# Moving the Q projection of eight token tiles from a fused attention/FFN kernel's K stage to the start of their FFN chunk

## The chip, the cores and the metric

The kernel runs on one core of a Trainium2 chip. The metric is the device time of one execution in microseconds. The core has TensorE for matmuls (PE in the profile, with PEld for its weight loads), VectorE (DVE) and ScalarE (ACT) for elementwise work, GpSimd (POOL), and SyncE (SP), whose queue issues the data transfers here. Matmul results go to PSUM, eight banks of 2 KB in each of 128 partitions; everything else lives in SBUF.

## The reference

One transformer block computes linear attention and a GeGLU feed-forward in parallel on the same normalized input; S = 2048 tokens, D = 576, 32 heads of 18, F = 4608, all in bf16:

```python
xn = layernorm(x)                       # over D, eps 1e-5
q, k, v = heads(xn @ wqkv)              # 32 heads of 18
phi = lambda t: where(t > 0, t + 1, exp(t)) + 1e-6
kv  = einsum("bhsd,bhse->bhde", phi(k), v)
z   = einsum("bhsd->bhd", phi(k))
num = einsum("bhqd,bhde->bhqe", phi(q), kv)
den = einsum("bhqd,bhd->bhq", phi(q), z)[..., None] + 1e-6
attn = merge_heads(num / den) @ wo
ffn  = (gelu(xn @ w_gate) * (xn @ w_up)) @ w_down
return x + attn + ffn
```

## The kernel before

The kernel works in two parts. In the **K stage** it goes over 16 tiles of 128 tokens. Each is normalized (statistics on VectorE, `rstd` on ScalarE, the scaling on either), transposed by a DMA (the first two by TensorE), projected to K and Q, and put through phi. From phi(K) it accumulates G = xn^T phi(K) in PSUM; a few steps after the last tile turn G and the V weights into the heads' kv products. Then come four **chunks** of 512 tokens. Each has 36 gate/up units (two outputs of 512 columns, gelu, product), and then the down projection of its four token tiles, into which the attention output is added.

The K and Q matmuls of a tile are ten each, of 288 columns: two halves of the 576 outputs, five blocks of the contraction. D = 576 is four blocks of 128 and a rest of 64, so the fifth block is half empty. Its row 64 (`HP`) holds ones on both sides, which adds 1 to the projection; phi is then max(t+1, min(exp(t), 1)), with the exponential's bias of -1:

```python
def kq_mm(n, which, hf):                        # which: 1 = K, 0 = Q
    c = which * D + hf * HALF
    for kt in range(KT):                        # KT = 5
        nc.tensor.matmul(                       # line 281
            ps_all[:, KQ_BANK[which] + hf, :HALF], lhsT=xnT[:, kt, n * P:(n + 1) * P],
            rhs=wqkv_sb[:, kt, c:c + HALF], start=(kt == 0), stop=(kt == KT - 1),
        )

def kq_exp(n, which, hf):                       # ScalarE, line 296
    ...activation(out=e, in_=ps_all[...], func=ACT.Exp, bias=neg1[:], scale=1.0)

def kq_phi(n, which, hf):                       # VectorE, line 301
    ...scalar_tensor_tensor(out=(pq, pk)[which][...], in0=e, scalar=1.0,
                            in1=ps_all[...], op0=ALU.min, op1=ALU.max)

def g_accumulate(n, pieces):                    # line 320; seven matmuls a tile in the K stage
    ...matmul(ps_all[:, b, col:col + w], lhsT=xn[:, n, kt * P:(kt + 1) * P],
              rhs=pk[:, n, 1 + d0:1 + d0 + w], ...)

def z_add(n):                                   # GpSimd, line 210: running sum of phi(K)
    ...tensor_tensor(out=z_sum, in0=z_sum, in1=pk[:, n, 1:D + 1], op=ALU.add)
```

`pk` has one column of ones on each side of a tile's phi(K), from which G also gets its column sums. Two matmuls of 289 columns a tile (`g_strip`, line 327) do G's 64-row rest.

The order in which the K stage's steps are given to the engines comes from a greedy model (`in_order`) with a duration for each step; a list `HEAD` fixes the first part of the order, up to about tile 5. Each engine runs its own steps in that order. Names in the list: `s` statistics, `a` aggregate, `r` rstd, `n` norm, `b` its bias, `t` a TensorE transpose, `c` the transposed tile, `m n.w.h` the matmuls of tile n, K (w = 1) or Q (w = 0), half h; `e` exponential, `p` phi, `z` the sum, `G`, `x` a load of two tiles, `w` warm-up matmuls.

The gate/up units run on two row tiles of TensorE: the upper and lower 64 rows of the array each hold their own weights, and two matmuls run side by side into two banks. For the rest of 64 rows, the lower half of the fifth block is a copy of the upper one:

```python
class _Unit:
    def p1(self):                               # first = (4, 0, 1, 2, 3): five pairs
        for kt in self.first:
            self.mm(0, LO, kt, ...)             # line 351
            last = self.mm(1, HI, kt, ...)
        self.turn = self.relay.nop()            # waits for `last`
    def p2(self):                               # then = (0, 1, 2, 3): four pairs, banks swapped
        for kt in self.then:
            m = self.mm(1, LO, kt, ...)         # the first waits for self.turn
            self.mm(0, HI, kt, ...)

def gu_pair(sc, k):                             # cut
    for i in range(GUB):                        # GUB = 2 units
        u = _Unit([bank a, bank b], lhs, rhs, nc.sync if blk == 0 else nc.gpsimd)
        u.p1()
    for each unit:
        u.p2()
        gelu on ScalarE (679), product to hT on VectorE (680)
    one job of den_jobs                         # phi(Q) -> normalized, transposed pqT
```

`den_jobs` uses phi(Q) of four tiles in each chunk, those of the chunk itself. After the K stage the transfers are issued in this order on one queue:

```python
load_w(2)                                       # V weights
nc.sync.dma_start(wqkv_sb[HP:P, 4, 2 * D:], A_wqkv[512:576, 2 * D:])
for i in range(NWBUF):                          # four blocks of gate/up weights
    load_gu(i, 0)
    load_gu(i, 1)
for c0, c1 in ((0, SC), (SC, S)):               # line 600
    nc.sync.dma_start(xnT[HP:P, 4, c0:c1], xnT[0:HP, 4, c0:c1])
for n in range(NS - 2):
    g_accumulate(n, G_B)                        # the fourth block's G
g_accumulate(NS - 1, G_A)
...                                             # copies of G, strips, kv products
```

At the end of each chunk but the last the tiles 2 and 3 of the down projection get one pair of matmuls (line 738) and then their adds on VectorE (764).

Of the kernel before, what the change touches and what calls it, by code (L numbers as in the profile page):

```python
# [15 lines left out]
P = 128  # L16
# [24 lines left out]
XW = 640  # L41
KLO = HP + 1
Q_CUT = 3
PKW = 578


class _Ring:
# [11 lines left out]
def kernel(  # L59
# [119 lines left out]
    nc.gpsimd.memset(xn[:, :, D:XW], 0.0)  # L179
    nc.gpsimd.memset(xn[:, :, D:D + 1], 1.0)  # L180
    nc.gpsimd.memset(wqkv_sb[HP:HP + 1, 4, 0:2 * D], 1.0)
    nc.gpsimd.memset(pk[:, :, 0:1], 1.0)
    nc.gpsimd.memset(pk[:, :, D + 1:D + 2], 1.0)

    bmask = const.tile([P, CR], F32, name="bmask")
    g_sb = apool.tile([P, KT, D], BF16, name="g_sb")
# [21 lines left out]

    def z_add(n):
        nc.gpsimd.tensor_tensor(  # L210
            out=z_bf[:] if n == NS - 1 else z_sum[:], in0=pk[:, 0, 1:D + 1] if n == 1 else z_sum[:], in1=pk[:, n, 1:D + 1],
            op=ALU.add,
        )

# [84 lines left out]

    def kq_phi(n, which, hf):  # L300
        nc.vector.scalar_tensor_tensor(  # L301
            out=(pq, pk)[which][:, n, which + hf * HALF:which + (hf + 1) * HALF], in0=e_tiles[n, which, hf][:], scalar=1.0,
            in1=ps_all[:, KQ_BANK[which] + hf, :HALF], op0=ALU.min, op1=ALU.max,
        )

    G_A = {
# [3 lines left out]
    }  # L312
    G_B = {3: [(4, 0, 0, 288), (5, 0, 288, 289)]}
    STRIP = ((6, 0, 1, 0), (7, HALF + 1, 0, HALF))
    eps_sum = const.tile([P, KT], F32, name="eps_sum")

    def g_accumulate(n, pieces):
        for kt, ps_ in pieces.items():
            for b, col, d0, w in ps_:
                nc.tensor.matmul(  # L320
                    ps_all[:, b, col:col + w], lhsT=xn[:, n, kt * P:(kt + 1) * P], rhs=pk[:, n, 1 + d0:1 + d0 + w],
                    start=(n == 0 and col == 0), stop=(n == NS - 1), skip_group_check=True,
                )

    def g_strip(n):
        for rows, (b, c0, _, _) in zip((LO, HI), STRIP):
            nc.tensor.matmul(  # L327
                ps_all[rows, b, 0:HALF + 1], lhsT=xn[:, n, 4 * P:D], rhs=pk[:, n, c0:c0 + HALF + 1],
                start=(n == 0), stop=(n == NS - 1), skip_group_check=True,
            )  # L330

# [126 lines left out]
    def step(name, *args, **kw):  # L458
        steps[name] = _Step(*args, **kw)

    GL = 0.0
    NORM = "DDDAADADADADADAD"
    COPY = ("DVE", "ACT")
    LEAD = (-9.0, 0.5, -0.5, -0.5)
    X_AT = [3.35, 4.40, 6.30, 8.80] + [10.40] * 4
# [4 lines left out]
    for n in range(NS):  # L470
        lead = LEAD[n] if n < 4 else 0.0
        after_x = [("x", n // 2 * 2)] if n >= 8 else []
        x_at = X_AT[n] if n < 8 else 0.0
        for h in range(2):
            step(("stats", n, h), "DVE", 0.40, n - 2.2 + lead, after_x, lambda n=n, h=h: ln_half(n, h), ready=x_at, tail=0.02)
        step(("aggr", n), "DVE", 0.14, n - 2.1 + lead, [("stats", n, 0), ("stats", n, 1)], lambda n=n: ln_aggr(n), tail=0.07)
        step(("rstd", n), "ACT", 0.43, n - 2.1 + lead, [("aggr", n)], lambda n=n: ln_rstd(n), tail=0.07)
        if n < TD:
            for i, (k0, k1, eng) in enumerate([(0, 3, "ACT"), (3, KT, COPY[n])]):
                b = TP_BANK[n] - i  # L480
                if NORM[n] == "A":
                    if not i:
                        step(("bias", n), "POOL", 0.20, n - 2.1 + lead, [("rstd", n)], lambda n=n: ln_bias(n))
                    step(("norm", n, i), "ACT", (0.49, 0.36)[i], n - 2.1 + lead, [("bias", n)],
                         lambda n=n, k0=k0, k1=k1: ln_norm_act(n, k0 * P, min(k1 * P, D)))
                else:
                    step(("norm", n, i), "DVE", (0.26, 0.19)[i], n - 2.1 + lead, [("rstd", n)],
                         lambda n=n, k0=k0, k1=k1: ln_norm(n, k0 * P, min(k1 * P, D)), tail=0.05)
                step(("tp", n, i), "PE", (0.32, 0.21)[i] if n == 0 else (0.18, 0.12)[i], n - 1.5 + lead, [("norm", n, i)],
                     lambda n=n, k0=k0, k1=k1, b=b: transposes(n, k0, k1, b), tail=0.08)  # L490
                step(("xnT", n, i), eng, 0.27 if i else 0.44, n - 0.88 + lead, [("tp", n, i)],
                     lambda n=n, k0=k0, k1=k1, b=b, eng=eng: tp_copy(n, k0, k1, b, acopy if eng == "ACT" else vcopy), tail=0.04)
            ready = [("xnT", n, 0), ("xnT", n, 1)]
        else:
            if NORM[n] == "P":
                step(("norm", n), "POOL", 2.35, n - 2.1 - GL, [("rstd", n)], lambda n=n: ln_norm_pool(n))
            elif NORM[n] == "A":
                step(("bias", n), "POOL", 0.15, n - 2.1, [("rstd", n)], lambda n=n: ln_bias(n))
                step(("norm", n), "ACT", 0.77, n - 2.1, [("bias", n)], lambda n=n: ln_norm_act(n), tail=0.09)
            else:  # L500
                step(("norm", n), "DVE", 0.36, n - 2.1, [("rstd", n)], lambda n=n: ln_norm(n), tail=0.07)
            step(("xnT", n), "SP", 2.10, n - 1.9, [("norm", n)], lambda n=n: dma_transposes(n), tail=2.05)
            ready = [("xnT", n)]
        for which, rank in ((1, n), (0, n + 0.6)):
            for h in range(2):
                r = rank + h / 100
                free = [("phi", n - 1, which, h)] if n else []
                if n == which == 0:
                    k0, k1 = ((0, Q_CUT), (Q_CUT, KT))[h]
                    step(("mm", 0, 0, h), "PE", 0.246 * (k1 - k0), r, ready + [("mm", 0, 0, 0)][:h],  # L510
                         lambda k0=k0, k1=k1: q_first(k0, k1), ready=W_AT[0][h], tail=0.15)
                else:
                    step(("mm", n, which, h), "PE", 0.615, r, ready + free, lambda n=n, w=which, h=h: kq_mm(n, w, h),
                         ready=W_AT[which] if which else W_AT[0][1], tail=0.15)
                step(("exp", n, which, h), "ACT", 0.46, r + 0.10, [("mm", n, which, 1 if n == which == 0 else h)],
                     lambda n=n, w=which, h=h: kq_exp(n, w, h), tail=0.03)
                step(("phi", n, which, h), "DVE", 0.37, r + 0.15, [("exp", n, which, h)],
                     lambda n=n, w=which, h=h: kq_phi(n, w, h), tail=0.08)
        if n > 0:
            idle = [("bias" if NORM[n + 4] == "A" else "norm", n + 4)] if n + 4 < NS else []  # L520
            step(("z", n), "POOL", 1.40, n + 2.0, [("phi", m, 1, h) for m in (0, n) for h in range(2)] + idle + ([("z", n - 1)] if n > 1 else []),
                 lambda n=n: z_add(n))
        step(("G", n), "PE", 0.75, n + 1.15, [("phi", n, 1, 0), ("phi", n, 1, 1)], lambda n=n: g_accumulate(n, G_A))
# [5 lines left out]
    def in_order(steps):  # L529
# [15 lines left out]
        return [name for _, _, name in sorted(begun)]  # L545

    HEAD = """
        s0.1 s0.0 a0 r0 s1.1 n0.0 t0.0 n0.1 t0.1 s1.0 a1 w c0.1 s2.0 c0.0 s2.1 m0.1.1 a2 r1 r2 m0.1.0 n1.1 e0.1.1
        t1.1 n1.0 n2 p0.1.1 m0.0.0 t1.0 B s3.0 e0.1.0 s3.1 a3 m0.0.1 c1.1 c1.0 e0.0.0 r3 m1.1.1 p0.1.0 p0.0.0 s4.1
        G0 m1.1.0 e0.0.1 s4.0 b3 c2 g n3 c3 e1.1.1 s5.0 p0.0.1 m1.0.0 e1.1.0 a4 p1.1.1 m1.0.1 s5.1 r4 p1.1.0 e1.0.0  # L550
        a5 m2.1.1 b4 e1.0.1 s6.0 m2.1.0 x8 s6.1 G1 n4 p1.0.0 e2.1.0 p1.0.1 m2.0.0 a6 e2.1.1 s7.0 p2.1.0 r5 m2.0.1
        p2.1.1 n5 z1 m3.1.0 c4 r6 s7.1 e2.0.1 e2.0.0 m3.1.1 G2 c5 p2.0.1 e3.1.0 a7 p2.0.0 p3.1.0 s8.0 b6 e3.1.1
        p3.1.1 z2 m3.0.1 s8.1 n6 a8 e3.0.1 s9.0 m3.0.0 c6 e3.0.0 G3 p3.0.1 s9.1 r7 a9 x10 n7 r8 m4.1.0 e4.1.0 x12
        m4.1.1 e4.1.1 m4.0.1 z3 r9 p3.0.0 m4.0.0 c7 p4.1.0 e4.0.1 p4.1.1 e4.0.0 n9 m5.1.0 p4.0.1 G4 b8 z4 m5.1.1 n8
        e5.1.0 c9
    """
    KIND = {
        "x": "x", "s": "stats", "a": "aggr", "r": "rstd", "b": "bias", "n": "norm", "t": "tp", "c": "xnT", "m": "mm",
# [87 lines left out]
    def gu_pair(sc, k):  # L646
# [29 lines left out]
        for i, (b, u) in enumerate(units):  # L676
# [4 lines left out]
            if den_jobs and i == 1 and 0 < k < NF // GUB - 1:  # L681
                job, n = den_jobs.pop(0)
                job(n)

    def m_product(c, bank):
        rows = DH * HCH[c]
        for hf in range(2):
# [80 lines left out]
                nc.sync.dma_start(out_view[:, self.n, :], self.res[:])  # L768

    for sc in range(NSC):  # L770
        for k in range(NF // GUB):
            gu_pair(sc, k)
            if sc == 0 and k in m_last_steps:
                m_last_steps[k]()
        while wd_loaded[0] < NF:
            load_wd_slice()

        tiles = [_DownTile(sc * TPC + j) for j in range(TPC)]
        tiles[0].pair()
        tiles[1].pair()  # L780
# [2 lines left out]
        for j, t in enumerate(tiles):  # L783
# [44 lines left out]
```

## Time and profile before

The time is 512.04 us (three executions, 512.02 to 512.2); the profiled execution spans 510.4 us.

| engine | busy us | share | what it mostly does |
|---|---|---|---|
| PE (TensorE) | 505.7 | 99% | pairs of gate/up, down projection, K and Q |
| PEld (weight loads) | 304.6 | 60% | runs beside PE |
| DVE (VectorE) | 212.7 | 42% | product of gate/up; statistics and phi in the K stage |
| ACT (ScalarE) | 137.0 | 27% | gelu; exponentials in the K stage |
| POOL (GpSimd) | 25.9 | 5% | sum of phi(K) |

A few groups of instructions matter for what follows (duration of one, from the page and the groups of the first 66 us): K/Q matmul 286 ns, 310 of them on line 281 and 10 on line 289 (the first tile's Q); exponential of 128x288 497 ns; phi 448 ns; statistics 444 ns; norm of 576 columns 860 ns on ScalarE and 696 ns on VectorE; sum of phi(K) on GpSimd 1249 ns; transposing DMA 1.2 us of issue and 2.6 us to landing.

A busy time is the sum of the recorded durations, with overlaps counted once. Instructions on one engine are pipelined: the next one starts before the record of the one before has ended, so the distance from start to start is what an instruction costs in a row. The chain of waits is followed back from the last instruction, at each step to what released it; a piece of it is the time by which the end would move if that piece alone went away and nothing else came in its place. A line such as 351 is that of a helper: gate/up and other units share it and are told apart by the tiles they read.

### The profile page before, as it was taken

How to read it: one execution, taken by the hardware profiler on the slowest of the kernel's cores; microseconds unless marked ns; L12 is line 12 of the kernel's file. 1: busy time of each engine (PE TensorE's matmuls, PEld its weight loads, DVE VectorE, ACT ScalarE, POOL GpSimd, SP SyncE). 2: the span in 40 equal slices, each digit the busy share in tenths (PEclk: the TensorE clock that was granted, in tenths of full speed). 3: DMA queues.
4: the chain of work that ended last, by engine and by line, in shares of the span. 5: the costliest groups of instructions: out<-in, count | busy, mean ns of one | idle time of the engine just before them, and what ended most of it. 6: DMA issues, size and time to landing. Idle time of an engine off the chain costs nothing.

```text
span 510.4 us, 10676 instructions
## 1 busy us (share of the span) xinstructions
PE 505.7 (99%) x4489; PEld 304.6 (60%) x4489; DVE 212.7 (42%) x449; ACT 137.0 (27%) x267; POOL 25.9 (5%) x40
## 2 busy tenths in 40 slices
PE   8999999999999999999999999999999999999997
PEld 7888854444587744444677644444777444445774
DVE  7996455555400045565210255555100356544101
ACT  6996523332400022322100023223000232232000
POOL 3444200000000000000000000000000000000000
PEclk9999999999999999999999999999999999999999
DMA  6747329999400067665300256567000556550000
GB/s 211 149 88 199 93 86 269 286 275 280 132 13 12 1 182 164 151 170 164 84 12 13 72 166 173 156 175 160 27 12 1 146 159 168 162 128 14 13 12 24
DMA packets 119162, 61.26 MB, mean 120 GB/s; under 512 B 25730, under 2 KB 118410, under 8 KB 119114
## 3 DMA queue, kind: packets, MB, share of 16 engines
q1 hardware_dynamic: 118970, 60.43, 45.4%
q8 instruction: 35, 0.57, 0.5%
q10 hardware_dynamic: 144, 0.15, 0.1%
q14 instruction: 13, 0.11, 0.1%
HBM read 52.86 MB, written 2.36 MB: 108 GB/s over the span
## 4 chain that ended last, share of the span: by engine, by line
PE 98%; DVE 1%; ACT 0%; DMA 0%; issue 0%
PE ps_all L351 55%; PE ps_all L750 28%; PE ps_all L281 7%; PE ps_all L320 3%; PE ps_all L755 3%; DMA x_sb<-in_A_x_dram 0%; PE ps_all L738 0%; PE ps_all L327 0%; DVE stats L224 0%; PE ps_all L400 0%; PE ps_all L690 0%; ACT phi_e L296 0%; ACT xnT L270 0%; DVE mv L227 0%; DVE xn L245 0%; ACT rstd L231 0%
## 5 line engine op out<-in xcount | busy, mean ns | idle before, releaser
L351 PE MATMUL ps_all<-xnT,wg 64*128 64x512 bf16 x1152 | 272.1, 376 | 0.0
L351 PE MATMUL ps_all<-xnT,wu 64*128 64x512 bf16 x1152 | 271.6, 376 | 0.0
L679 ACT ACTIVATE gl<-ps_all 128x512 f32<-128x512 f32 x144 | 86.0, 597 | 308.9 <-PE ps_all L351 308.8
L680 DVE TENSOR_TENSOR hT<-ps_all,gl 128x512 bf16<-128x512 f32 x144 | 99.6, 692 | 130.8 <-ACT gl L679 130.4
L351 PEld LDWEIGHTS <-wu 64*128 64x128 bf16 x1152 | 108.3, 94 | 68.1
L351 PEld LDWEIGHTS <-wg 64*128 64x128 bf16 x1152 | 108.3, 94 | 67.8
L750 PE MATMUL ps_all<-wd_sb,hT 128*128 128x288 bf16 (+2 forms) x1152 | 147.1, 286 | 0.0
L750 PEld LDWEIGHTS <-hT 128*128 128x128 bf16 x1152 | 110.9, 98 | 30.9 <-issue 1.3
L764 DVE TENSOR_TENSOR res<-ps_all,x_sb 128x288 bf16<-128x288 f32 (+2 forms) x32 | 13.8, 455 | 146.3 <-PE ps_all L755 88.1
L351 PE MATMUL ps_all<-xnT,wr 64*128 64x512 bf16 x288 | 54.6, 376 | 0.0
L281 PE MATMUL ps_all<-wqkv_sb,xnT 128*128 128x288 bf16 x310 | 40.7, 286 | 0.1
L281 PEld LDWEIGHTS <-xnT 128*128 128x128 bf16 x310 | 29.5, 98 | 7.3 <-ACT xnT L270 0.4
L296 ACT ACTIVATE phi_e<-ps_all,neg 128x288 f32<-128x288 f32 x64 | 30.7, 497 | 9.2 <-PE ps_all L281 6.2
L351 PEld LDWEIGHTS <-wr 64*128 64x128 bf16 x288 | 14.0, 94 | 16.7
L755 PE MATMUL ps_all<-m_sb,pqT 128*128 128x288 bf16 (+2 forms) x128 | 20.9, 286 | 0.0
L320 PE MATMUL ps_all<-hT,xn 128*128 128x288 bf16 (+4 forms) x144 | 18.8, 274 | 0.0
L210 POOL TENSOR_TENSOR z_sum<-z_sum,hT 128x576 f32<-128x576 f32 x13 | 16.2, 1249 | 18.5 <-DVE hT L301 17.8
L301 DVE SCALAR_TENSOR_TENSOR pq<-phi_e,ps_all 128x288 bf16<-128x288 f32 x32 | 14.1, 448 | 6.1 <-ACT phi_e L296 6.0
L320 PEld LDWEIGHTS <-xn 128*128 128x128 bf16 x144 | 13.9, 98 | 3.9 <-DVE hT L301 0.3
L301 DVE SCALAR_TENSOR_TENSOR hT<-phi_e,ps_all 128x288 bf16<-128x288 f32 x32 | 14.0, 448 | 2.6 <-ACT phi_e L296 2.4
L755 PEld LDWEIGHTS <-pqT 128*128 128x128 bf16 x128 | 12.4, 98 | 3.3
L224 DVE BATCH_NORM_STATS2 stats<-x_sb 128x6 f32<-128x288 bf16 x32 | 13.4, 444 | 1.1 <-DMA x_sb<-in_A_x_dram 1.1
(70 smaller groups left out, 130.7 us busy)
## 6 DMA issues: line engine op xcount, KB each, us to landing
wg<-in_B_w_gate_dram SPq DMA_DIRECT2D x72, 256.0 KB, 2.9
wu<-in_B_w_up_dram SPq DMA_DIRECT2D x72, 256.0 KB, 3.6
wd_sb<-in_B_w_down_dram SPq DMA_DIRECT2D x12, 432.0 KB, 4.8
wr<-in_B_w_gate_dram SPq DMA_DIRECT2D x72, 32.0 KB, 2.9
wr<-in_B_w_up_dram SPq DMA_DIRECT2D x72, 32.0 KB, 3.1
out_dram<-res SPq DMA_DIRECT2D x15, 144.0 KB, 1.8
wqkv_sb<-in_A_wqkv_dram SPq DMA_DIRECT2D x2, 576.0 KB, 4.5
x_sb<-in_A_x_dram SPq DMA_DIRECT2D x4, 288.0 KB, 3.6
```

The source lines that it names most:

```text
L210: nc.gpsimd.tensor_tensor(out=z_bf[:] if n == NS - 1 else z_sum[:], in0=pk[:, 0, 1:D + 1] if n == 1 else z_sum[:], in1=pk[:, n, 1:D + 1], ...
L224: nc.vector.bn_stats(out=ln_raw[n][:, h, :], in_=x_sb[:, n, h * HALF:(h + 1) * HALF])
L281: nc.tensor.matmul(ps_all[:, KQ_BANK[which] + hf, :HALF], lhsT=xnT[:, kt, n * P:(n + 1) * P], rhs=wqkv_sb[:, kt, c:c + HALF], start=(kt == ...
L296: nc.scalar.activation(out=e[:], in_=ps_all[:, KQ_BANK[which] + hf, :HALF], func=ACT.Exp, bias=neg1[:], scale=1.0,)
L301: nc.vector.scalar_tensor_tensor(out=(pq, pk)[which][:, n, which + hf * HALF:which + (hf + 1) * HALF], in0=e_tiles[n, which, hf][:], scala ...
L320: nc.tensor.matmul(ps_all[:, b, col:col + w], lhsT=xn[:, n, kt * P:(kt + 1) * P], rhs=pk[:, n, 1 + d0:1 + d0 + w], start=(n == 0 and col = ...
L351: return nc.tensor.matmul(self.outs[i], lhsT=self.lhs(i, rows, kt), rhs=self.rhs(i, rows, kt), start=start, stop=stop, skip_group_check=True,)
L679: nc.scalar.activation(out=gl[:], in_=ps_all[:, b[0], :], func=ACT.Gelu_apprx_tanh)
L680: nc.vector.tensor_tensor(out=hT[:, GUB * k + i, :], in0=ps_all[:, b[1], :], in1=gl[:], op=ALU.mult)
L750: nc.tensor.matmul(self.acc(hf), lhsT=hT[:, f, j * P:(j + 1) * P], rhs=wd_sb[:, f, self.parts[hf]], start=(f == 0 and not paired), stop=Fa ...
L755: nc.tensor.matmul(self.acc(hf), lhsT=pqT[:, c, self.ts], rhs=m_sb[:, c, self.parts[hf]], start=False, stop=(paired and c == 3), skip_grou ...
L764: nc.vector.tensor_tensor(out=self.res[:, hs], in0=self.acc(hf), in1=x_sb[:, self.n, hs], op=ALU.add)
```

## The change

Q of the tiles 6, 7, 9, 10, 11, 13, 14 and 15 is no longer computed in the K stage. It is computed at the start of the chunk to which the tile belongs (two tiles in chunk one, three each in chunks two and three), as units on two row tiles, like gate/up. The 64-row rest then is one pair. It uses no row of ones: phi is formed as max(t, 0) + min(exp(t), 1), with one more VectorE operation for each half. The Q weights are loaded a second time, into the buffer that held `wo`, after the first down tile of chunk zero. ScalarE loads its exponential table before the down projections of chunks zero to two, and that of gelu again after the late Q.

The whole K stage is now a fixed list of steps, with its Q halves of tiles 4, 5, 8 and 12 set behind later tiles' K. The model's number for the transposing DMA changes from 2.10 us to 1.25 (with a tail of 2.9 or 2.0 us), and the assignment of norms to engines becomes strictly alternating from tile 3. The store of phi(K) gets four columns of ones on each side instead of one, so that a tile begins on a multiple of four elements; G's last pieces and its strips take up to four columns of ones.

```diff
+LATE = (6, 7, 9, 10, 11, 13, 14, 15)
+PK0 = 4
-PKW = 578
+PKW = D + 2 * PK0
...                                             # pk[:, n, 1 + ...] -> pk[:, n, PK0 + ...] throughout
     G_A = {
-        0: [(0, 0, 0, 288), (1, 0, 288, 289)],
-        2: [(2, 0, 0, 288), (3, 0, 288, 289)],
-        1: [(0, 288, 0, 224), (1, 289, 224, 223), (2, 288, 447, 130)],
+        0: [(0, 0, 0, 288), (1, 0, 288, 292)],
+        2: [(2, 0, 0, 288), (3, 0, 288, 292)],
+        1: [(0, 288, 0, 224), (1, 292, 224, 220), (2, 288, 444, 136)],
     }
-    G_B = {3: [(4, 0, 0, 288), (5, 0, 288, 289)]}
+    G_B = {3: [(4, 0, 0, 288), (5, 0, 288, 292)]}
...                                             # strip: HALF + 1 columns -> HALF + PK0
-    NORM = "DDDAADADADADADAD"
+    NORM = "DDDADADADADADADA"
...
-        for which, rank in ((1, n), (0, n + 0.6)):
+        for which, rank in ((1, n), (0, n + 0.6))[:1 if n in LATE else 2]:
...
     HEAD = """
-        s0.1 s0.0 a0 r0 s1.1 n0.0 t0.0 n0.1 t0.1 s1.0 a1 w c0.1 s2.0 c0.0 s2.1 m0.1.1 a2 r1 r2 m0.1.0 n1.1 e0.1.1
-        t1.1 n1.0 n2 p0.1.1 m0.0.0 t1.0 B s3.0 e0.1.0 s3.1 a3 m0.0.1 c1.1 c1.0 e0.0.0 r3 m1.1.1 p0.1.0 p0.0.0 s4.1
-        G0 m1.1.0 ...                           # ends at tile 5; the model orders the rest
+        s0.1 s0.0 a0 r0 s1.1 n0.0 t0.0 n0.1 s1.0 a1 c0.0 t0.1 c0.1 s2.1 r1 s2.0 w m0.1.0 a2 m0.1.1 n1.1 t1.1 n1.0 r2
+        e0.1.0 t1.0 n2 m0.0.0 c1.1 p0.1.0 m0.0.1 s3.1 c1.0 s3.0 e0.1.1 e0.0.0 p0.1.1 e0.0.1 a3 m1.1.0 m1.1.1 r3
+        p0.0.0 b3 G0 ...
+        ... e8.1.1 s12.0 p8.1.1 a13 e8.1.0 p8.1.0 G7 n11 s15.1 p4.0.1 m9.1.1 m9.1.0 e5.0.0 e9.1.1 G8 e9.1.0 c10 s12.1
+        m5.0.1 z6 a12 p9.1.1 p9.1.0 m10.1.1 z7 r12 e5.0.1 p5.0.0 n12 r13 m10.1.0 c11 m8.0.0 ...
+        ... m12.0.0 p11.1.1 p11.1.0 m12.1.1 r14 m12.1.0 G10 n14 b15 e8.0.1 p8.0.1 m12.0.1 e12.1.1
+        e12.1.0 p12.1.1 m13.1.1 n15 p12.1.0 e13.1.1 m13.1.0 ... G12 m15.1.1 p12.0.1 m15.1.0 G13 G14 e15.1.1 e15.1.0
+        p12.0.0 p15.1.1 z13 p15.1.0 z14 z15
     """
...
+    class _LateQ:
+        def __init__(self, n):
+            two = [banks.next(), banks.next()]
+            self.n, self.acc = n, [ps_all[:, b, :HALF] for b in two]
+            self.unit = _Unit(
+                self.acc, lambda i, rows, kt: xnT[rows, kt, n * P:(n + 1) * P],
+                lambda i, rows, kt: wo2[rows, kt, i * HALF:(i + 1) * HALF], nc.gpsimd,
+            )
+        def phi(self):
+            for i, acc in enumerate(self.acc):
+                e = fwork.tile([P, SC], F32, name="gl")
+                nc.scalar.activation(out=e[:, :HALF], in_=acc, func=ACT.Exp)
+                nc.vector.tensor_scalar_min(out=e[:, :HALF], in0=e[:, :HALF], scalar1=1.0)
+                nc.vector.scalar_tensor_tensor(
+                    out=pq[:, self.n, ...], in0=acc, scalar=0.0, in1=e[:, :HALF], op0=ALU.max, op1=ALU.add,
+                )
+    def late_q(sc):
+        left = [n for n in LATE if n // TPC == sc]
+        while left:
+            qs = [_LateQ(n) for n in left[:2]]
+            left = left[2:]
+            for q in qs:
+                q.unit.p1()
+            for q in qs:
+                q.unit.p2()
+                q.phi()
+    def load_late_wq(): ...                     # Q weights -> wo2, three transfers
...
     for sc in range(NSC):
+        if any(n // TPC == sc for n in LATE):
+            late_q(sc)
+            nc.scalar.preload_act_table_set("gelu_apprx_tanh_and_others")
         ...                                     # gate/up
+        if any(n // TPC == sc + 1 for n in LATE):
+            nc.scalar.preload_act_table_set("natural_log_exp_and_others")
         ...                                     # down projection
+            if sc == j == 0:
+                load_late_wq()
```

More of the change, by code (lines that the diff above doesn't have):

```diff
@@ L181 @@
     nc.gpsimd.memset(wqkv_sb[HP:HP + 1, 4, 0:2 * D], 1.0)
-    nc.gpsimd.memset(pk[:, :, 0:1], 1.0)
-    nc.gpsimd.memset(pk[:, :, D + 1:D + 2], 1.0)
+    for c in (0, PK0 + D):
+        nc.gpsimd.memset(pk[:, :, c:c + PK0], 1.0)
     bmask = const.tile([P, CR], F32, name="bmask")
@@ L210, in z_add @@
         nc.gpsimd.tensor_tensor(
-            out=z_bf[:] if n == NS - 1 else z_sum[:], in0=pk[:, 0, 1:D + 1] if n == 1 else z_sum[:], in1=pk[:, n, 1:D + 1],
+            out=z_bf[:] if n == NS - 1 else z_sum[:], in0=pk[:, 0, PK0:PK0 + D] if n == 1 else z_sum[:], in1=pk[:, n, PK0:PK0 + D],
             op=ALU.add,
@@ L301, in kq_phi @@
         nc.vector.scalar_tensor_tensor(
-            out=(pq, pk)[which][:, n, which + hf * HALF:which + (hf + 1) * HALF], in0=e_tiles[n, which, hf][:], scalar=1.0,
+            out=(pq, pk)[which][:, n, PK0 * which + hf * HALF:PK0 * which + (hf + 1) * HALF], in0=e_tiles[n, which, hf][:], scalar=1.0,
             in1=ps_all[:, KQ_BANK[which] + hf, :HALF], op0=ALU.min, op1=ALU.max,
@@ L308 @@
     G_A = {
[3 rows of a table removed]
-    }
-    G_B = {3: [(4, 0, 0, 288), (5, 0, 288, 289)]}
-    STRIP = ((6, 0, 1, 0), (7, HALF + 1, 0, HALF))
[3 rows of a table added]
+    }
+    G_B = {3: [(4, 0, 0, 288), (5, 0, 288, 292)]}
+    STRIP = ((6, 0, PK0, 0), (7, PK0 + HALF, 0, HALF))
     eps_sum = const.tile([P, KT], F32, name="eps_sum")
@@ L320, in g_accumulate @@
                 nc.tensor.matmul(
-                    ps_all[:, b, col:col + w], lhsT=xn[:, n, kt * P:(kt + 1) * P], rhs=pk[:, n, 1 + d0:1 + d0 + w],
+                    ps_all[:, b, col:col + w], lhsT=xn[:, n, kt * P:(kt + 1) * P], rhs=pk[:, n, PK0 + d0:PK0 + d0 + w],
                     start=(n == 0 and col == 0), stop=(n == NS - 1), skip_group_check=True,
@@ L327, in g_strip @@
             nc.tensor.matmul(
-                ps_all[rows, b, 0:HALF + 1], lhsT=xn[:, n, 4 * P:D], rhs=pk[:, n, c0:c0 + HALF + 1],
+                ps_all[rows, b, 0:HALF + PK0], lhsT=xn[:, n, 4 * P:D], rhs=pk[:, n, c0:c0 + HALF + PK0],
                 start=(n == 0), stop=(n == NS - 1), skip_group_check=True,
@@ L501 @@
                 step(("norm", n), "DVE", 0.36, n - 2.1, [("rstd", n)], lambda n=n: ln_norm(n), tail=0.07)
-            step(("xnT", n), "SP", 2.10, n - 1.9, [("norm", n)], lambda n=n: dma_transposes(n), tail=2.05)
+            step(("xnT", n), "SP", 1.25, n - 1.9, [("norm", n)], lambda n=n: dma_transposes(n), tail=2.9 if n < 4 else 2.0)
             ready = [("xnT", n)]
-        for which, rank in ((1, n), (0, n + 0.6)):
+        for which, rank in ((1, n), (0, n + 0.6))[:1 if n in LATE else 2]:
             for h in range(2):
                 r = rank + h / 100
-                free = [("phi", n - 1, which, h)] if n else []
+                last = [m for m in range(n) if which or m not in LATE][-1:]
+                free = [("phi", m, which, h) for m in last]
                 if n == which == 0:
@@ L547 @@
     HEAD = """
-        s0.1 s0.0 a0 r0 s1.1 n0.0 t0.0 n0.1 t0.1 s1.0 a1 w c0.1 s2.0 c0.0 s2.1 m0.1.1 a2 r1 r2 m0.1.0 n1.1 e0.1.1
-        t1.1 n1.0 n2 p0.1.1 m0.0.0 t1.0 B s3.0 e0.1.0 s3.1 a3 m0.0.1 c1.1 c1.0 e0.0.0 r3 m1.1.1 p0.1.0 p0.0.0 s4.1
-        G0 m1.1.0 e0.0.1 s4.0 b3 c2 g n3 c3 e1.1.1 s5.0 p0.0.1 m1.0.0 e1.1.0 a4 p1.1.1 m1.0.1 s5.1 r4 p1.1.0 e1.0.0
-        a5 m2.1.1 b4 e1.0.1 s6.0 m2.1.0 x8 s6.1 G1 n4 p1.0.0 e2.1.0 p1.0.1 m2.0.0 a6 e2.1.1 s7.0 p2.1.0 r5 m2.0.1
-        p2.1.1 n5 z1 m3.1.0 c4 r6 s7.1 e2.0.1 e2.0.0 m3.1.1 G2 c5 p2.0.1 e3.1.0 a7 p2.0.0 p3.1.0 s8.0 b6 e3.1.1
@@ L553 @@
-        p3.1.1 z2 m3.0.1 s8.1 n6 a8 e3.0.1 s9.0 m3.0.0 c6 e3.0.0 G3 p3.0.1 s9.1 r7 a9 x10 n7 r8 m4.1.0 e4.1.0 x12
-        m4.1.1 e4.1.1 m4.0.1 z3 r9 p3.0.0 m4.0.0 c7 p4.1.0 e4.0.1 p4.1.1 e4.0.0 n9 m5.1.0 p4.0.1 G4 b8 z4 m5.1.1 n8
-        e5.1.0 c9
+        s0.1 s0.0 a0 r0 s1.1 n0.0 t0.0 n0.1 s1.0 a1 c0.0 t0.1 c0.1 s2.1 r1 s2.0 w m0.1.0 a2 m0.1.1 n1.1 t1.1 n1.0 r2
+        e0.1.0 t1.0 n2 m0.0.0 c1.1 p0.1.0 m0.0.1 s3.1 c1.0 s3.0 e0.1.1 e0.0.0 p0.1.1 e0.0.1 a3 m1.1.0 m1.1.1 r3
+        p0.0.0 b3 G0 e1.1.0 n3 s4.0 e1.1.1 m1.0.0 e1.0.0 p0.0.1 c2 m1.0.1 s4.1 p1.1.0 s5.0 m2.1.0 a4 e1.0.1 p1.1.1
@@ new lines @@
+        r4 s5.1 p1.0.0 B a5 e2.1.0 p1.0.1 m2.1.1 G1 e2.1.1 n4 m2.0.0 r5 m2.0.1 c3 p2.1.0 e2.0.0 p2.1.1 g e2.0.1 s6.0
+        s7.1 p2.0.0 s6.1 p2.0.1 G2 m3.1.1 b5 n5 x8 c4 a6 m3.1.0 s7.0 c5 e3.1.1 p3.1.1 z1 a7 m3.0.0 m3.0.1 m4.1.1
+        e3.1.0 r6 p3.1.0 s8.0 e3.0.0 m4.1.0 r7 e4.1.1 G3 n6 e4.1.0 x10 p3.0.0 b7 z2 s8.1 p4.1.1 e3.0.1 p4.1.0 a8
+        m4.0.0 p3.0.1 n7 r8 m5.1.1 m5.1.0 e5.1.1 e5.1.0 s9.1 s9.0 n8 c6 z3 e4.0.0 G4 a9 p5.1.1 p5.1.0 c7 r9 s11.0
+        m4.0.1 s11.1 m6.1.1 e6.1.1 s10.0 p6.1.1 m6.1.0 x12 e6.1.0 z4 a11 G5 p6.1.0 s10.1 p4.0.0 b9 a10 m7.1.1 m7.1.0
@@ new lines @@
+        n9 e7.1.1 e7.1.0 G6 p7.1.1 r10 r11 s13.1 x14 b11 m5.0.0 p7.1.0 n10 c8 z5 m8.1.1 s13.0 c9 m8.1.0 e4.0.1
+        e8.1.1 s12.0 p8.1.1 a13 e8.1.0 p8.1.0 G7 n11 s15.1 p4.0.1 m9.1.1 m9.1.0 e5.0.0 e9.1.1 G8 e9.1.0 c10 s12.1
+        m5.0.1 z6 a12 p9.1.1 p9.1.0 m10.1.1 z7 r12 e5.0.1 p5.0.0 n12 r13 m10.1.0 c11 m8.0.0 p5.0.1 s15.0 e10.1.1
+        e10.1.0 e8.0.0 a15 p10.1.1 p10.1.0 c12 b13 p8.0.0 m8.0.1 m11.1.1 z8 s14.0 n13 s14.1 e11.1.1 r15 m11.1.0 z9
+        e11.1.0 G9 a14 c13 m12.0.0 p11.1.1 p11.1.0 m12.1.1 r14 m12.1.0 G10 n14 b15 e8.0.1 p8.0.1 m12.0.1 e12.1.1
@@ L556 @@
+        e12.1.0 p12.1.1 m13.1.1 n15 p12.1.0 e13.1.1 m13.1.0 p13.1.1 e13.1.0 e12.0.0 G11 c14 z10 z11 m14.1.1 p13.1.0
+        m14.1.0 e14.1.1 e14.1.0 c15 z12 e12.0.1 p14.1.1 p14.1.0 G12 m15.1.1 p12.0.1 m15.1.0 G13 G14 e15.1.1 e15.1.0
+        p12.0.0 p15.1.1 z13 p15.1.0 z14 z15
     """
@@ L683, in gu_pair, with load_late_wq @@
                 job(n)
+    class _LateQ:
[12 more added lines that the diff above has]
+                nc.vector.scalar_tensor_tensor(
+                    out=pq[:, self.n, i * HALF:(i + 1) * HALF], in0=acc, scalar=0.0, in1=e[:, :HALF], op0=ALU.max, op1=ALU.add,
+                )
[9 more added lines that the diff above has]
+                q.phi()
+    def load_late_wq():
+        nc.sync.dma_start(wo2[:, 0:4, :], A_wqkv[0:512, 0:D].rearrange("(kt p) c -> p kt c", p=P))
+        for rows in (LO, HI):
+            nc.sync.dma_start(wo2[rows, 4, :], A_wqkv[512:576, 0:D])
     def m_product(c, bank):
```

## The prediction

> **What bounds the kernel now.** I read the page's chain first, because a change that moves work between stages is worth only what it takes from that chain:
>
> ```profile
> PE 98%; DVE 1%; ACT 0%; DMA 0%; issue 0%
> PE ps_all L351 55%; PE ps_all L750 28%; PE ps_all L281 7%; PE ps_all L320 3%; PE ps_all L755 3%; DMA x_sb<-in_A_x_dram 0%; PE ps_all L738 0%; PE ps_all L327 0%; DVE stats L224 0%; PE ps_all L400 0%; PE ps_all L690 0%; ACT phi_e L296 0%; ACT xnT L270 0%; DVE mv L227 0%; DVE xn L245 0%; ACT rstd L231 0%
> ```
>
> TensorE carries the end for 98% of the span, from about 9.4 us on. Line 281 is the K and Q matmuls, 320 the G matmuls, 351 every row-tiled pair, 750 the down projection. So the change is worth what it does to TensorE's work, plus any hole it opens. Next the chain in order of time, for two tiles of the K stage and the end of it:
>
> ```profile
> 37.42 2.45 PE ps_all L281 x20
> 39.87 0.75 PE ps_all L320 x7
> ...
> 56.63 1.23 PE ps_all L281 x10
> 57.86 4.27 PE ps_all L320 x35
> 62.13 2.11 PE ps_all L327 x32
> 64.23 0.61 PE ps_all L320 x4
> 64.84 1.11 PE ps_all L400 x20
> ...
> 66.46 70.28 PE ps_all L351 x652
> ```
>
> The columns are start, length and piece. A tile costs 2.45 us for 20 K/Q matmuls (0.1225 each) and 0.75 for 7 G matmuls, with nothing between pieces. The stretches by engine show how close the others are:
>
> ```profile
> core 0: us, PE busy (x) PEld busy (x) DVE busy (x) ACT busy (x) POOL busy (x), PEclk, DMA share, GB/s
> 9.40:20.00 10.60, 10.52 (x88) 8.34 (x89) 10.43 (x34) 9.90 (x26) 5.20 (x9) 1.00 0.48 92
> 20.00:30.00 10.00, 10.00 (x87) 8.08 (x85) 9.02 (x26) 9.00 (x25) 4.53 (x6) 1.00 0.70 158
> 30.00:40.00 10.00, 10.00 (x87) 8.11 (x85) 9.82 (x25) 8.94 (x24) 4.30 (x5) 1.00 0.40 80
> 40.00:50.00 10.00, 10.00 (x86) 8.13 (x85) 6.31 (x15) 6.40 (x13) 3.69 (x3) 1.00 0.79 209
> ```
>
> To 40 us VectorE is busy 9 to 10.4 us of each ten and ScalarE about 9, mostly because the layer norms run ahead; after that both are at two thirds. Shortening TensorE's share here therefore leans on engines with little room.
>
> **What the Trainium skill says, and whether this trace agrees.** "TensorE: Matmul & The Clock Gate", Back-to-back issue gap, gives N/2.4 + 2.5 ns for a warm matmul of N columns: 122.5 ns for 288 columns, as here (2.45 us / 20), and 215.8 for 512. "TensorEngine Tiling (Array Packing)", Key Properties, says that row tiles work independently, in parallel. The trace agrees: a chunk's 36 units of gate/up are 18 matmuls of 512 columns each (648), and in the chunks after the first they take 69.93 us; 69.93 / 36 = 1.94 us is nine slots of 0.216, not eighteen. The same page, Restrictions and Gotchas, says that two row tiles cannot use one PSUM bank at once; the kernel keeps to that by swapping banks between its two passes, with a relay on another engine between. "GPSIMD Engine Reference", Specifications, says that GpSimd shares its SBUF interfaces with VectorE. Here VectorE's 576-column norm takes 0.43 us at 30.03, and 1.23 and 1.55 at 34.89 and 38.29, when a z addition starts on GpSimd within 0.15 us of it.
>
> **The change, part by part.**
>
> *Removed from the K stage.* Eight tiles lose their ten Q matmuls: 8 x 10 x 0.1225 = **-9.80 us** of TensorE. With them go 16 exponentials (about 0.40 us from start to start in a back-to-back run) and 16 phi operations (about 0.36).
>
> *Added before gate/up.* A late Q tile is one unit of two outputs: pass one has five pairs, pass two four, so nine slots instead of ten, because the 64-row remainder of the contraction is one pair and no longer costs a full matmul. Nothing shows that 288 columns pair worse than 512: the two pairs of line 738 are 288 columns wide and are followed by gate/up 0.26 us after their start:
>
> ```profile
> 287.05 0.42 PE L738 MATMUL ps_all<-m_sb,pqT 64*128 64x288 bf16 x4
> 287.19 0.10 PEld L351 LDWEIGHTS <-wr 64*128 64x128 bf16 x2
> 287.31 0.38 PE L351 MATMUL ps_all<-xnT,wr 64*128 64x512 bf16 x2
> ```
>
> So 8 x 9 x 0.1225 = **+8.82 us**. Removing and adding together is -0.98 us: a tenth of the moved work, 0.2% of the time. Everything else must be weighed against that one microsecond.
>
> *The relay.* Pass two of a unit may start only when the last matmul of pass one is through and a no-op on GpSimd has passed it on. A matmul record is 0.286 us in a slot of 0.1225, so its end comes 0.16 after its slot; a hand-over between engines shows as 0.02 to 0.05 of issue in the chain of the first 10 us, there are two of them, and the no-op itself I guess at 0.05. Estimate 0.30 us. With two tiles side by side the other tile's pass one (5 x 0.1225 = 0.61) covers it. But chunks two and three have three late tiles each, so the third goes alone: 2 x 0.30 = **+0.6 us**. The before kernel never runs a nine-slot unit alone.
>
> *Wider G and strip operands.* The aligned K store has four ones columns on each side instead of one: a tile's seven G matmuls grow from 1731 to 1740 columns, 9/2.4 ns x 16 tiles = 0.06 us; the strip by 3 columns x 32 = 0.04; the fourth block's G by 3 x 16 = 0.02. **+0.13 us**, rounded up.
>
> *The fixed list, start.* TensorE idles 0.39 us before the matmul at 9.44 for the copy of tile 1 on ScalarE, and 0.2 before G at 10.27. The new list puts only one exponential ahead of that copy instead of two, and two K halves ahead of G0: **-0.35 us**.
>
> *The fixed list, middle.* A tile without Q takes 1.2 + 0.75 = 1.98 us of TensorE. From starts of neighbours in the trace VectorE needs 2 x 0.37 (statistics) + 0.13 + 2 x 0.36 (phi) + half a norm at 0.36 = 1.77; ScalarE 2 x 0.40 + 0.43 + half of 0.77 = 1.62. Adding up the list up to each step, VectorE's work stays within about 1 us of TensorE's until tile 9, and VectorE starts 2 us earlier (statistics at 3.29, first transposes at 5.4). That holds unless a norm meets a z addition; two of the seven norms did, at about 1 us each. Part of that gets through: **+0.4 us**.
>
> *The end of the K stage.* The DMA queue issues its last loads after the last transpose:
>
> ```profile
> 41.12 0.57 SPq L109 DMA_DIRECT2D wqkv_sb<-in_A_wqkv_dram  x1
> ...
> 52.98 5.38 SPq L600 DMA_DIRECT2D xnT<-xnT  x2
> ```
>
> From the first load to the first copy of the 64-row remainder (line 600) are 11.86 us of issue. That copy feeds the very first pair of gate/up. Now there are 13.5 us from 52.98 to there. In the list the norm of tile 15 sits on ScalarE behind the exponentials of tile 12, which puts the last transpose at about 42.5, the first copy at 54.4 and its landing near 56.5; gate/up would begin at 66.46 - 9.80 - 0.35 + 0.13 = 56.4. A near tie: **+0.1 us**.
>
> *Beside the path.* Late phi adds to VectorE, per tile, two minima (estimate 0.25 us) and two phi (0.45), 1.4 us, and two exponentials to ScalarE; gate/up holds VectorE at 37 of 70 us and ScalarE at 21. The adds of the last two down tiles take 1.55 us, and the banks they free are asked for only after two late tiles (2.2 us). Table loads are 1.28 us each; the one to exponentials falls in the down stage. In chunk zero it starts at about 137.3 and delays a copy at 138.24 by 0.4, whose bank is used again only at 139.88. The 0.66 MB of late weights load during the first down stage, where the page's slices show 1 to 13 GB/s. All **0**.
>
> *Sum.* -9.80 + 8.82 + 0.60 + 0.13 - 0.35 + 0.40 + 0.10 = -0.10: 512.04 becomes **511.9 us**.
>
> **Rivals.**
> *Everything hides.* The relay passes in the shadow, the list opens no hole: -9.80 + 8.82 + 0.13 - 0.35 = -1.2, so 510.8. For it: the new list spreads the postponed Q halves of tiles 4, 5, 8 and 12 as filler where K waits. Against it: the lone third tiles have nothing to fill with.
> *VectorE becomes the bound of the K stage.* If four or five norms collide with z and each microsecond arrives at TensorE, the stage gets 2 us back: about 513.5. For it: 9 to 10.4 us busy in ten already. Against it: sixteen phi less, and long instructions overlap, so busy time overstates the load.
> *The remainder's copy or a transpose takes the wait's place.* Each further microsecond by which tile 15's transpose is late is a microsecond before gate/up: 512.5 to 513.5. For it: transposes take 1.2 us of issue and 2.6 to land, and tiles now pass in 1.98. Against it: only tiles 6, 7, 9 to 11 and 13 to 15 pass that fast.
>
> **Range and chances.** Working steps are precise to about 0.1 us, but the holes are not: the best case is 1.2 below before, and two holes together give 1.6 above. I take 510.8 to 513.5. Both ends are within 0.3% of 512.04, so a change over 2% (10 us) would need a stage to break; 1% each way.
>
> **What would show it.** In the profile after: 80 fewer records on the K/Q line and 144 more on the pair line; the first gate/up pair near 56.5 us; TensorE waits within the K stage under 0.5 us in all; each late pair of tiles 2.2 us long before gate/up of chunks one to three, and a hole of about 0.3 us in the middle of the third tile in chunks two and three. It is wrong if the K stage shows holes naming VectorE or a transpose of over 1 us, if pairs of 288 columns take more than 0.1225 each, or if gate/up's first pair waits for the copy.

## The result, and the profile after

The changed kernel takes 514.5 us (median of six executions, 513.81 to 516.83) against 512.2 (512.02 to 512.3): a ratio of 1.0052, 95% interval 1.0033 to 1.0071. The forecast was 511.9, range 510.8 to 513.5: about 2.6 us too fast, and outside its own range.

The page's chain says at once what is new. It was TensorE for 98%, with no transfer to speak of:

```profile
PE 96%; DMA 2%; DVE 1%; ACT 0%; issue 0%; POOLq 0%
```

The waits of TensorE in the changed kernel name the transfers (what waited, for whom, microseconds in all, times, longest). The first two lines below had no counterpart before; the kernel before has only two start-up waits:

```profile
engine line waited for: us in total, times, longest us
PE ps_all L353 <- DMA xnT<-xnT: 1.5, 1, 1.5
PE ps_all L283 <- DMA xnT<-xn: 1.3, 1, 1.3
```

Lines have moved by two: 353 is the pair line (351 before), 283 the K/Q line (281). The chain in order of time shows where they lie:

```profile
24.57 5.61 DMA xnT<-xn
...
30.22 1.40 PE ps_all L283 x10
...
47.75 5.72 PE ps_all L322 x49
...
55.56 4.06 DMA xnT<-xnT
...
59.66 70.26 PE ps_all L353 x647
...
170.89 72.14 PE ps_all L353 x684
...
282.92 2.84 PE ps_all L353 x46
...
285.78 0.03 POOLq L362
...
285.86 70.59 PE ps_all L353 x656
```

The first piece is the transpose of tile 8, which took 5.6 us to land; tile 8's K waited for it. The fourth is the copy of the 64-row rest for tiles 0 to 3, which feeds the first pair of gate/up. The last four lines are chunks one and two with their late Q in front, to be compared with this chunk of the kernel before:

```profile
177.64 69.93 PE ps_all L351 x648
```

The K stage was to win nearly ten microseconds of TensorE; gate/up ran on at 59.66 instead of 66.39, so 6.7 were won. The chunks give back 2.21 + 3.60 + 3.60 = 9.4. A recorded wait begins only at the modelled end of the matmul before it, and that is later than the end of its slot: by slots, TensorE lost 1.4 us before tile 8 (28.80 to 30.22) and 1.9 before gate/up (57.74, where the first matmul of the pair went, to 59.66).

### The profile page after: what moved, and what is told of

It is laid out like the page before. It is cut to its first block, busy times and chain, and to the rows that moved or that the text cites. A ratio compares the mean times of both kernels' runs of the same rounds, so it can differ in the third digit from the quotient of the medians.

```text
span 512.7 us, 10826 instructions
## 1 busy us (share of the span) xinstructions
PE 505.4 (99%) x4553; PEld 309.3 (60%) x4553; DVE 215.5 (42%) x465; ACT 142.6 (28%) x273; POOL 26.3 (5%) x40
## 4 chain that ended last, share of the span: by engine, by line
PE 96%; DMA 2%; DVE 1%; ACT 0%; issue 0%; POOLq 0%
PE ps_all L353 56%; PE ps_all L796 28%; PE ps_all L283 5%; PE ps_all L801 3%; PE ps_all L322 3%; DMA xnT<-xn 1%; DMA xnT<-xnT 1%; DMA x_sb<-in_A_x_dram 0%; PE ps_all L784 0%; PE ps_all L329 0%; DVE stats L226 0%; PE ps_all L291 0%; PE ps_all L268 0%; PE ps_all L736 0%; PE ps_all L142 0%
## 5 line engine op out<-in xcount | busy, mean ns | idle before, releaser
L353 PE MATMUL ps_all<-xnT,wu 64*128 64x512 bf16 x1152 | 268.1, 376 | 0.0
L353 PEld LDWEIGHTS <-wu 64*128 64x128 bf16 x1152 | 107.0, 94 | 65.7
L353 PE MATMUL ps_all<-xnT,wr 64*128 64x512 bf16 x288 | 61.8, 376 | 1.5 <-DMA xnT<-xnT 1.5
L709 ACT ACTIVATE gl<-ps_all 128x288 f32<-128x288 f32 x16 | 5.9, 411 | 119.0 <-PE ps_all L353 117.0
L283 PE MATMUL ps_all<-wqkv_sb,xnT 128*128 128x288 bf16 x230 | 31.0, 287 | 1.3 <-DMA xnT<-xn 1.3
L353 PEld LDWEIGHTS <-wr 64*128 64x128 bf16 x288 | 17.2, 94 | 16.0
L283 PEld LDWEIGHTS <-xnT 128*128 128x128 bf16 x230 | 21.9, 98 | 6.7 <-DMA xnT<-xn 1.6
L298 ACT ACTIVATE phi_e<-ps_all,neg 128x288 f32<-128x288 f32 x48 | 22.9, 497 | 7.1 <-PE ps_all L283 5.4
```

Of the source, the lines that this page charges most:

```text
L283: nc.tensor.matmul(ps_all[:, KQ_BANK[which] + hf, :HALF], lhsT=xnT[:, kt, n * P:(n + 1) * P], rhs=wqkv_sb[:, kt, c:c + HALF], start=(kt == ...
L298: nc.scalar.activation(out=e[:], in_=ps_all[:, KQ_BANK[which] + hf, :HALF], func=ACT.Exp, bias=neg1[:], scale=1.0,)
L353: return nc.tensor.matmul(self.outs[i], lhsT=self.lhs(i, rows, kt), rhs=self.rhs(i, rows, kt), start=start, stop=stop, skip_group_check=True,)
```

## The experiments

**e1: the copy first.**

```diff
+    nc.sync.dma_start(xnT[HP:P, 4, 0:SC], xnT[0:HP, 4, 0:SC])
     load_w(2)
     ...                                        # V rest, four gate/up blocks
-    for c0, c1 in ((0, SC), (SC, S)):
-        nc.sync.dma_start(xnT[HP:P, 4, c0:c1], xnT[0:HP, 4, c0:c1])
+    nc.sync.dma_start(xnT[HP:P, 4, SC:S], xnT[0:HP, 4, SC:S])
```

> The first copy of the 64-row rest (tiles 0 to 3) is issued ahead of the V and gate/up loads instead of behind them; nothing else changes. Theory A (two transfers that arrive late took the wait's place: the copy 1.53 us, a transpose 1.26 us): the wait of gate/up's first pair goes, -1.5 us, so about 513.0. Theory B (VectorE and ScalarE are too slow for the shortened K stage, and the transfers only carry their lateness): the wait moves into the strips or kv products, 514.0 to 514.5.

Measured: 512.57 us (ratio to the kernel before 1.0008, interval 1.0000 to 1.0017), 1.9 under the changed kernel. The copy's wait is gone, gate/up starts at 57.55, no wait on VectorE or ScalarE takes the place, and tile 8's wait is still there at 1.2 us. The reduction is the slot distance of 1.9, not the recorded 1.5.

**c1: the same edit in the kernel before.**

> The kernel before, with the first copy of the 64-row rest issued ahead of the V and gate/up loads, as in e1. If the copy's wait exists only because the K stage became shorter, this does nothing: 512.2, since before the copy was issued at 53.0 us and needed at 66.4. If the copy's place in the queue costs in itself, this is faster by about as much as e1 was against the changed kernel, 1.5 us.

Measured: 511.95 us (ratio 1.0000, interval 0.9992 to 1.0009). There the copy is issued 13 us before gate/up needs it, and nothing waits for it. So its place in the queue costs nothing by itself; the shorter K stage made it the wait that ends last.

**e2: tile 8's transpose ahead of a load.**

```diff
-  ... r11 s13.1 x14 b11 m5.0.0 p7.1.0 n10 c8 z5 ...
+  ... r11 s13.1 b11 m5.0.0 p7.1.0 n10 c8 x14 z5 ...
```

> The load of x tiles 14 and 15 is issued just after tile 8's transpose instead of just before it. Theory A (tile 8's transpose landed after 5.6 us instead of 2.6 because it stood behind two loads of 288 KB): TensorE's wait of 1.26 us before tile 8's K goes wholly or nearly; the copy's wait stays or grows by up to that amount where the last transposes don't come earlier with it; 513.2 to 514.4. Theory B (VectorE had tile 8's norm late): tile 8's K waits as before, 514.4.

Measured: 516.27 us (ratio 1.0077, interval 1.0061 to 1.0093), slower than the changed kernel and outside both expectations. Its waits:

```profile
PE ps_all L353 <- DMA xnT<-xnT: 3.0, 1, 3.0
...
PE ps_all L283 <- DVE hT L303: 0.3, 1, 0.3
```

Tile 8's wait did go: the transposes between 20 and 34 us now land in 3.3 us at most. TensorE reached gate/up earlier, but the copy did not come earlier (issued at 55.51), so the whole gain came back as wait. Part of that is one transpose, the last, whose issue took 2.4 us instead of 1.2 in this profile; why is open. The rest of the loss is in the stretches after the wait (the clock is the number behind the five engines):

```profile
60.30:62.00 1.70, 1.70 (x13) 0.76 (x14) 0.00 (x0) 0.00 (x0) 0.00 (x0) 0.72 0.00 0
62.00:64.00 2.00, 2.00 (x12) 0.91 (x10) 0.00 (x0) 0.00 (x0) 0.00 (x0) 0.50 0.00 0
64.00:66.00 2.00, 2.00 (x18) 0.97 (x16) 0.15 (x1) 0.60 (x1) 0.00 (x0) 0.88 0.00 0
```

TensorE stood for 3.0 us and then ran at half its clock: 12 matmul records in 2 us where a full-speed stretch has 22. The gate/up of chunk zero took 71.94 us instead of 70.26, 1.7 more. The clock missing in the three stretches accounts for it: 0.28 x 1.70 + 0.50 x 2.00 + 0.12 x 2.00 = 1.7 us.

**e8 and e9: what a hole costs.** Both are e4 (below) with the copies behind the loads again. e8 puts the larger copy first; e9 instead loads 1 MB of gate/up weights a second time ahead of them:

```diff
+    for i in (2, 3):                           # e9: same data, same place
+        nc.sync.dma_start(wg[:], B_w_gate[...]); nc.sync.dma_start(wu[:], B_w_up[...])
```

> e4, but with both copies behind the loads and the larger one first, so that gate/up waits longer: a hole of 3 to 5 us. If a hole costs its length alone, the time is 510.9 plus the hole. If TensorE's clock falls after it, as in the look at e2 (hole 3.0 us, clock 0.50 to 0.88 until 66 us), the granted clock after the hole is down again to about a half for 2 to 4 us and the time is 1.5 to 2.5 us more than that: 515.5 to 518.

> e4 with both copies behind the loads, and 1 MB of gate/up weights loaded a second time ahead of them (the same data to the same place), so that gate/up's wait becomes clearly longer than the 1.8 us of e8: 4 to 6 us. If a hole costs only its length, the time is 510.9 plus the hole and the granted clock stays at 1.00. If a long hole lowers the clock, as the look at e2 (3.0 us) suggests, the clock in the few us after it falls to about 0.5 and the time is another 1.5 to 2.5 us longer.

e8 (one execution): 512.66 us, a wait of 1.8 us instead of the 3 to 5 expected. Gate/up went on at 58.21, 1.9 us later than in e4, and ran at full clock:

```profile
60.00:62.00 2.00, 2.00 (x22) 1.06 (x20) 0.00 (x0) 0.58 (x1) 0.00 (x0) 1.00 0.00 0
```

That is e4's 510.94 plus 1.9, 512.8. Putting the larger copy first did not lengthen the wait beyond what the runs with it second show (1.0 to 3.0 us). e9 (one execution): 518.96 us, a wait of 5.8 us, and these stretches:

```profile
56.00:61.00 5.00, 0.61 (x7) 0.26 (x6) 1.48 (x3) 0.00 (x0) 0.57 (x1) 0.83 0.96 251
61.00:63.00 2.00, 0.56 (x4) 0.30 (x5) 0.00 (x0) 0.00 (x0) 0.00 (x0) 0.50 0.17 36
63.00:65.00 2.00, 2.00 (x14) 0.75 (x10) 0.00 (x0) 0.00 (x0) 0.00 (x0) 0.50 0.00 0
65.00:67.00 2.00, 2.00 (x16) 0.90 (x14) 0.00 (x0) 0.00 (x0) 0.00 (x0) 0.73 0.00 0
```

The clock falls inside the hole and comes back only near 66 us. Gate/up goes on at 62.44, 6.1 us later than in e4, and in chunk zero takes 72.04 us, 1.8 more: 510.94 + 6.1 + 1.8 = 518.8. So in the profiles a hole recorded as 1.5 or 1.8 us cost its length, one of 3.0 or 5.8 its length and another 1.7 to 1.8.

**e3: three late tiles side by side.**

```diff
-            qs = [_LateQ(n) for n in left[:2]]
-            left = left[2:]
+            qs = [_LateQ(n) for n in left[:3]]
+            left = left[3:]
```

> Chunks two and three run all three late tiles side by side: three first passes, then three second passes. Both theories: the two relay holes of 0.29 us go, -0.6 us, about 513.9; if the third tile's banks aren't free yet after two first passes, a new wait on the adds of VectorE appears instead.

Measured: 516.29 us (514.5 to 518.47; ratio 1.0078, interval 1.0053 to 1.0103). As a time this run does not answer its question: its edit lies behind the K stage, but tile 8's wait was 2.0 us in the profile and the copy's 1.0 (1.3 and 1.5 in the changed kernel), and the mean clock of its executions goes from 1.000 down to 0.993. The chain answers it: chunks two and three take 73.36 us each instead of 73.53, so 0.17 is saved in each, not 0.29. Twenty-seven slots on top of 69.93 would be 73.24; the missing 0.12 shows in e4's trace, where the second unit of gate/up starts one of its row tiles 0.15 us behind the other, in the bank that the first late tile's last phi gives free at that moment.

**e4: the three edits together.**

> The three edits of e1, e2 and e3 together. Theory A: 514.5 - 1.5 - 1.3 - 0.6 = 511.1, that is about 1 us under the kernel before. Theory B: a wait on VectorE or ScalarE takes the place of the transfers', 512.5 or more.

Measured: **510.94 us** (510.55 to 511.16; ratio 0.9973, interval 0.9963 to 0.9984), 3.6 under the changed kernel and 1.2 under the kernel before. All that TensorE waits for:

```profile
PE ps_all L142 <- DVE x_sb L120: 1.1, 1, 1.1
PE ps_all L268 <- DVE xn L247: 0.5, 1, 0.5
```

These are the start-up waits of before; gate/up starts at 56.31. VectorE is busy 9.25 us of the ten from 30 to 40 and lets nothing wait. Theory A predicted 511.1; theory B had 512.5 or more.

**e7: the second copy later.** The changed kernel, with the copy for tiles 4 to 15 put off into chunk zero.

> The changed kernel, with the second copy of the 64-row rest (tiles 4 to 15, 192 KB) put off into chunk zero; the first stays behind the loads. If the first copy landed late (4.1 us after its issue, against some 2 before) because the second shares the transfer engines with it, it now lands in about 2 us and gate/up's wait falls from 1.5 us to nearly nothing. If the gate/up loads ahead of it are the cause, the wait stays at 1 to 2 us.

One execution: 513.37 us; the first copy lands 3.5 us after issue instead of 4.1 and gate/up waits 1.0 us. The second copy is at most a part of it, and even that is not shown: the other profiles with the copy behind the loads (e9 aside) spread from 3.7 to 4.7 us, more than this difference.

**e5: Q of all twelve tiles late.** e4 with `LATE` = 4 to 15, the steps of the Q halves of 4, 5, 8 and 12 struck from the list.

> e4 with Q of tiles 4, 5, 8 and 12 moved out as well (all of chunks one to three; at most three tiles side by side), their steps struck from the fixed list, the rest of its order kept. By slots alone: 4 x 0.1225 = 0.5 us less than e4, 510.45. Theory A (transfers are what the short tiles run into): a tile passes in 1.98 us from tile 4 on, transposes still need 1.2 us of issue and 2.6 to land, and without the filler halves TensorE waits for transposes; 511 to 513. Theory B (VectorE and ScalarE): it waits for phi or exponentials, naming those engines, 511 to 514.

Measured: 513.35 us (ratio 1.0025, interval 1.0017 to 1.0033), 2.4 slower than e4. Both theories were half right:

```profile
PE ps_all L283 <- DVE hT L303: 1.2, 3, 0.5
PE ps_all L283 <- DMA xnT<-xn: 1.2, 1, 1.2
```

Removing another 40 matmuls (4.9 us) brought gate/up forward by only 1.6 us, from 56.31 to 54.72, while the late units cost their slots: 74.34 us for a chunk of four. Without filler halves the K stage does wait for VectorE and for a transpose.

**e6: the list of before.** e4, with the list and norm assignment of the kernel before; the model orders the rest.

> e4, but with the list and the norms' engines of the kernel before, so that the greedy model orders all from about tile 5 on: what the fixed list is worth. If the list matters (it spreads the Q halves of tiles 4, 5, 8 and 12 as filler and puts norms ahead), TensorE waits for transposes or phi in the K stage, 1 to 3 us: 512 to 514. If late Q alone does it, the same as e4, 511.

Measured: 512.26 us (ratio 1.0009, interval 1.0002 to 1.0016), 1.3 slower than e4; beside e4 the kernel before took 512.19 us, beside e6 511.99. In its chain VectorE carries most of 22 to 33 us, including this norm that met a z addition:

```profile
30.98 1.22 DVE xn L247
```

TensorE waits 0.5 us behind it, and gate/up starts 1.3 us later than in e4. The fixed list is worth about what the whole change earns.

## Why the prediction was wrong

Of its three signs of being wrong two came: a hole of over 1 us in the K stage that names a transpose, and gate/up's first pair waiting for the copy.

**Held.** The pairs: 72.14 - 69.93 = 2.21 us for two late tiles is 18 slots of 0.1225, so 288 columns pair as well as 512, and 8.82 was right. The relay: 3.60 - 27 x 0.1225 = 0.29 for a tile alone, against 0.30. Late phi, table loads and late weights lie beside the path; no wait names them. The wider G leaves no trace: seven matmuls are still 0.75 us.

**Start, somewhat mis-sized.** -0.35 was forecast. G0 ends at 11.61 with tile 1's second K half already done; before, it ended at 11.20 with that half (0.61) still to come. That is -0.2.

**Failed: "The fixed list, middle", +0.4 us.** It added up the work of VectorE and ScalarE and left out when a transpose lands; where the prediction names that time, it is 2.6 us without regard to the queue. The DMA queue of the changed kernel shows what it missed:

```profile
23.43 1.04 SPq L96 DMA_DIRECT2D x_sb<-in_A_x_dram  x2
24.57 19.16 SPq L275 DMA_TRANSPOSE xnT<-xn  x8
```

Two loads of 288 KB are issued just ahead of tile 8's transpose, which then landed in 5.6 us. Moving only the second load behind it (e2, e4) takes the wait away: the transpose then lands in 3.3 us. TensorE lost 1.4 us here. The kernel before already held the sign, at tile 7, in its queue and in the landing times of its transposes:

```profile
20.03 1.04 SPq L94 DMA_DIRECT2D x_sb<-in_A_x_dram  x2
21.17 4.21 SPq L273 DMA_TRANSPOSE xnT<-xn  x3
...
DMA to landing us min/median/max: 2.6/2.6/4.0
```

The longest, 4.0 us, is the one issued at 21.17 behind two loads; TensorE did not wait for it. That VectorE could have become the bound was not empty: e5 and e6 show it, but not this list with eight tiles late.

**Failed: "The end of the K stage", +0.1 us.** The copy was forecast to be issued at 54.4: 42.5, the time forecast for the last transpose, plus 11.86 us of loads. The last transpose did start at 42.53, but its own 1.2 us of issue come before the first load (43.79), so the copy went at 55.56. Taken as a start, 42.5 came true by luck: without tile 8's hole (e8) that transpose starts at 40.80, the first copy goes at 53.61, and TensorE reaches gate/up at 56.00. The landing was mis-sized: 2.1 us, read from where the traffic after the copy's issue ends in the kernel before, against 4.1 measured. The end of the traffic is too early a mark. In e7 (copy issued at 55.12) it ends by 58.0, 2.9 us after the issue, and the copy lands at 58.6 (the last number is GB/s):

```profile
57.50:58.00 0.50, 0.17 (x1) 0.00 (x0) 0.50 (x2) 0.00 (x0) 0.45 (x1) 1.00 0.07 18
58.00:58.50 0.50, 0.00 (x0) 0.00 (x0) 0.50 (x2) 0.00 (x0) 0.12 (x1) 1.00 0.00 0
```

Why the queue cleared in 2.1 us in the kernel before and only in 2.9 in e7 is open: the same loads stand ahead of the copy in both. That the copy's place behind them made the wait is shown (e1). The rival that put a copy or a transpose in the place of the wait named the right mechanism, though through a late transpose of tile 15, and gave it 512.5 to 513.5; both a transpose and the copy were waited for, one after the other, for 3.3 us where the sum had allowed 0.5.

The corrected sum is -9.80 + 9.41 - 0.2 + 1.4 + 1.9 = +2.7. At the last down projection the chains differ by 2.64; the profiled spans by 2.3 (512.7 and 510.4), since the last store of the kernel before took 0.3 longer in its profile.

**The range was too narrow for another reason.** It treated a hole as its length. One of the six executions took 516.83 us at a mean clock of 0.997, while the others lie between 513.81 and 514.99. That execution has no trace here, so the link to e2 and e9 is an inference.

## What to carry to other kernels

When work leaves a stage bound by one engine, go through every transfer needed at the new, earlier point and ask when it can land, with what is queued ahead of it; a landing time read from a quiet stage does not hold behind loads. Issue the small transfer that the next stage needs first ahead of the large ones that it needs later. And a small saving in slots, 1 us here, is real only when no hole opens: the same change is 2.3 us slower or 1.2 us faster by the place of two transfers in a queue and one grouping.

## What the runs showed of the hardware

A TensorE pause of about 3 us cost more than itself. The Trainium skill, "TensorE: Matmul & The Clock Gate", Part 1: The HAM clock gate, says that an idle window of about 3.4 us halves the clock, and that the window runs free of the kernel. The runs agree: 0.50 after pauses of 3.0 and 5.8 us, none after 1.5 and 1.8, and 1.7 to 1.8 us lost each time beyond the pause. The recorded 3.0 us of e2 are 3.4 us from the start of the last matmul before it (56.85) to the next (60.24), so it is at the edge of such a window, and whether a pause of that length is caught may differ from execution to execution.

The landing time of a transfer from SBUF to SBUF varied with what was queued before it. A transpose took 2.6 us alone, 3.3 when one load of 288 KB stood just ahead (e2, e4, e8; 3.9 in e5), and with two of them ahead 3.6 to 4.0 in the order of the kernel before (with c1 and e6) and 5.5 to 6.3 in the changed kernel, e1 and e3. A copy of 64 KB took 2.0 to 3.1 us ahead of the V and gate/up loads (e5, e6, e1, e4, c1) and 3.5 to 4.7 behind them (the changed kernel, e2, e3, e7, e8). The spread at one place in the queue is wide, so these figures give a direction and not a rule.
